# VectorE's sum of an attention output's two halves, moved ahead of the tail copy and the score passes of its step

## The chip, the cores and the metric

The kernel runs on one core of a Trainium2 chip. The metric is the device time of one execution in microseconds (us). Five engines work side by side, each through its own list of instructions in order: PE (TensorE, matmuls; its weight loads are listed as PEld), DVE (VectorE), ACT (ScalarE), POOL (GpSimd) and SP (SyncE, which issues the DMAs).

## What is computed

Attention with a learned position bias over 4 batches and 8 heads, 576 positions of 64 dimensions, then two feed-forward stages over the 2304 resulting rows of 512. Everything is float32.

```python
scores = scale * np.matmul(q, k.transpose(0, 1, 3, 2))
...
scores = scores + bias.transpose(2, 0, 1)[None, :, :, :]
scores = scores - np.max(scores, axis=-1, keepdims=True)
attn = np.exp(scores)
attn = attn / (np.sum(attn, axis=-1, keepdims=True) + 1e-09)
return np.matmul(attn, v).astype(np.float32)
...
h = np.maximum(np.maximum(x @ w1, x @ w2), x @ w3)
return (h @ w_out).astype(np.float32)
...
h = x @ w_in
g = np.where(h > 0.0, h, alpha * (np.exp(np.minimum(h, 0.0)) - 1.0))
return (g @ w_out).astype(np.float32)
```

## The kernel before

The program has four stretches: the bias table (up to about 48 us), attention (about 48 to 300 us), the first feed-forward stage (to about 620 us) and the second.

Attention goes through 16 pairs of a head pair and a batch, `n`. Each pair takes five steps `c` = 0 to 4, one for each block of query rows: four blocks of 128 rows for both heads, then a last step in which the 64 remaining rows of both heads share 128 partitions. Step number `s` is 5 `n` + `c`. Rows are called here by `c`: step c0, step c1 and so on.

In a step, PE multiplies queries and keys into two PSUM tiles `pb` (`unit_qk`, L240 and L245, one tile for each head). DVE adds the bias, takes the row minimum and writes the scores `e_t` with its minima `st_t` (`scores`, L255, one pass for each head, so two passes in steps c0 to c3 and one in c4). ACT takes the exponential in place (`expo`, L261). Two steps later PE transposes that block in 64-row pieces (`trans`, L299) into the two PSUM tiles `tq`, and ACT copies these out to SBUF (`evac`, L80); in the steps in which the block is c0 or c2, DVE copies the second of the two (L82, 128x512). The last 64 columns of a block are "tails": they are transposed into the edges of the first `pb` tile, ahead of the step's queries times keys, and DVE copies them out (`evac_tails`, L82, 128x128 or 64x128). The row sums of a half are inverted on DVE (`recip`, L276 and L277), transposed on PE, and copied out on DVE (`rows_out`, L283).

The products with the values (`pv`, L366, L370, L374) are collected in two PSUM tiles `xo`, over a half of the pair: blocks 0 and 1 (256 rows), or blocks 2, 3 and 4 (320 rows). The two `xo` tiles hold two halves of one sum. When a half is complete, ACT copies the first tile to SBUF (`x_copy`, L388, tile `xf`), DVE adds the second to it (`x_sum`, L392), and POOL multiplies by the inverted row sums (L393) and splits the result into two parts (L78, L86). PE may write the second `xo` tile for the next half only after DVE has added it. The sum of the 256-row half stands in step c2, that of the 320-row half in step c0 of the next pair.

Between these, `pump` issues pieces of the decoding of the later stages' weights, four pieces for each pair (in every step but c1): DVE operations L468, L471, L473, L475, L478 in turn, ACT operations L470 and L80 (`w_t`, `sp`), and a POOL subtraction.

The order on every engine is that in which the program issues its instructions. A list `plan` holds each call with a key, the step number plus an offset, and the calls are issued in the order of the keys (`at`, and the loop at its end). Within a step the keys that matter here are: queries times keys at .00 and .01, the tail copy at .015, the copy of the inverted sums at .016, the passes over the scores at .02 and .03, the inversion at .025, decoding at .32, and exponentials and copies of `tq` from .38 to .40. `x_sum` is at `X_AT` + 0.427 = 6.027 of the step that completed the half, so at .027 of a step.

Of the kernel before, what the change touches and what calls it, by code (L numbers as in the profile page):

```python
# [38 lines left out]
X_AT = {1: 5.6, 4: 5.6}  # L39
# [15 lines left out]
def fused_kernel(ctx, tc, tkq, vv, lt, pk, wm1, wo1, win2, wo2, out):  # L55
# [79 lines left out]
    with ExitStack() as pro:  # L135
# [57 lines left out]
        for A in range(36):  # L193
# [20 lines left out]
            c, r = divmod(A, 8)  # L214
# [381 lines left out]
    def at(key, fn, *args):  # L596
        plan.append((key, len(plan), fn, args))

    for s, (n, c) in enumerate(steps):
        o = {nm: s + off for nm, off in OFF.items()}  # L600
        at(o["qk0"], unit_qk, s, 0)
        at(o["t0"], scores, s, 0)
        at(o["ex0"], expo, s, 0)
        if c < 4:
            at(o["qk1"], unit_qk, s, 1)
            at(o["t1"], scores, s, 1)
            at(o["ex1"], expo, s, 1)
        if c in (1, 4):
            at(s + 1.025, recip, s)
            at(s + (2.205 if end else 1.995), sums, s)  # L610
            at(s + (2.312 if end else 2.016), rows_out, s)
        at(o["tr"], trans, s)
        end = s > NS - 3
        at(s + 1.98, places, s)
        at(s + (2.20 if end else 1.99), tails, s)
        at(o["ev0"], evac, s, 0)
        at(o["ev1"], evac, s, 1)
        at(s + (2.311 if end else 2.015), evac_tails, s)
        if c in (1, 4):
            for off, k in PV_AT[c]:  # L620
                at(s + off + 0.01 * k, pv, s, k)
            at(s + R_AT, load_r, s)
            at(s + X_AT[c], x_copy, s)
            at(s + X_AT[c] + 0.427, x_sum, s)
            at(s + X_AT[c] + 0.5, x_hi, s)
            at(s + X_AT[c] + 0.75, x_lo, s)
        if s > 5 and c != 1:
            at(o["pump"], pump)
        if n % 4 == 3 and n < 15:
            at(s + 0.45, load_b, n // 4 + 1, c)  # L630
# [122 lines left out]
    def small(tag, bufs):  # L753
        return mp.tile([128, NB], F32, tag=tag, name=f"{tag}_t", bufs=bufs)
# [61 lines left out]
    with tc.manual_schedule():  # L816
        for n, u in enumerate(units + [None]):
# [6 lines left out]
            if n < 2:  # L824

                for i in range(2):
                    w = take_w(("wi", u[1], 3 * i))
                    v = take_w(("w3", pre[1], i)) if pre else None
                    for q, (b, d) in enumerate(((B11, B21), (B12, B22))):
# [3 lines left out]
                        c = small("c", 4)  # L833
# [121 lines left out]
```

## Time and profile before

| | |
|---|---|
| time, median of 3 runs | 989.96 us (989.78 to 994.21) |
| the profiled execution's own time | 990.71 us |
| its span, first to last instruction | 988.9 us |
| mean granted TensorE clock | 0.998 |
| busy over the span: PE, DVE, ACT, POOL | 98%, 68%, 52%, 32% |
| busy in 142.3 to 158.0 us, one pair of attention (15.7 us): PE, DVE, ACT | 15.51, 12.56, 12.59 us |

The profile is of one execution. Its time lies 1.8 us over its span, since the span leaves out what is ahead of the first and behind the last instruction. PE's busy time counts matmuls with modelled ends, which lie over one another; a PE that is called busy may still be held up. In attention PE, DVE and ACT are all used for most of the time, and behind it PE alone sets the pace.

### The profile page before, as it was taken

To read this page: it belongs to the slowest core of one execution; us is meant where nothing else is said; L and a number is where in the kernel's file an instruction comes from. 1 tells how busy PE (TensorE), PEld (TensorE's weight loads), DVE (VectorE), ACT (ScalarE), POOL (GpSimd) and SP (SyncE) were. 2 spreads that over 40 slices of the span, in tenths; PEclk is the share of its full clock that TensorE was granted. 3 is DMA by queue.
4 is the path that set the end of the run, shared out by engine and by line. 5 is a ranking of instruction groups with operands and counts; after the bars stand their busy time and mean duration, and the time that the engine had idled before them with its cause. 6 is when DMAs were issued, how large, how long until landed. Compare 5 with 4: busy or idle time off the path is not lost.

```text
span 988.9 us, 19965 instructions
## 1 busy us (share of the span) xinstructions
PE 969.5 (98%) x7492; PEld 820.6 (83%) x7492; DVE 675.6 (68%) x1374; ACT 516.1 (52%) x1076; POOL 320.9 (32%) x307
## 2 busy tenths in 40 slices
PE   7989999999999999999999999999999999999998
PEld 4656666666658999999999999989899998989996
DVE  8968788888784899878978933745763456643342
ACT  8877778777872433334333324443454434444343
POOL 0003333334333555435534520322323233222322
PEclk9999999999999999999999999999999999999999
DMA  7965756657534468789978961465567655676563
GB/s 243 303 213 161 222 180 216 191 159 243 149 102 136 174 184 301 247 296 329 311 262 277 323 224 43 127 185 184 186 212 236 200 181 179 205 245 198 177 190 106
DMA packets 80416, 205.23 MB, mean 208 GB/s; under 512 B 13360, under 2 KB 29504, under 8 KB 80320
## 3 DMA queue, kind: packets, MB, share of 16 engines
q1 hardware_dynamic: 80320, 203.96, 63.3%
q8 instruction: 59, 0.97, 0.4%
q14 instruction: 37, 0.30, 0.1%
HBM read 155.21 MB, written 48.72 MB: 206 GB/s over the span
## 4 chain that ended last, share of the span: by engine, by line
PE 92%; DVE 3%; DMA 2%; ACT 2%; issue 0%; POOL 0%; SPq 0%; ACTq 0%
PE xo L750 18%; PE pb L794 13%; PE pb L574 12%; PE xo L366 8%; PE tq L794 7%; PE pb L240 6%; PE xo L574 5%; PE tq L574 5%; PE pb L674 4%; PE tq L299 3%; PE xo L674 2%; PE tq L674 2%; DMA scr<-o_t 2%; PE pb L299 2%; PE xo L370 2%; PE pb L204 1%
## 5 line engine op out<-in xcount | busy, mean ns | idle before, releaser
L86 POOL TENSOR_TENSOR gl<-t_t,gh 128x384 fp32r<-128x384 f32 x96 | 108.8, 1144 | 286.0 <-ACT gh L80 286.0
L261 ACT ACTIVATE e_t<-e_t,st_t 128x576 f32<-128x576 f32 x144 | 111.3, 773 | 54.3 <-DVE st_t L255 46.2
L794 PE MATMUL pb<-w_t,gh 128*128 128x512 f32 x384 | 119.3, 392 | 0.0
L574 PE MATMUL pb<-xh,w_t 128*128 128x384 f32 x448 | 116.9, 336 | 0.0
L750 PE MATMUL xo<-tt,w_t 128*128 128x384 f32 x528 | 107.4, 338 | 0.0
L255 DVE CUSTOM_DVE_ANT_0 e_t<-pb,b_t 128x576 f32<-128x576 f32 x144 | 105.0, 744 | 2.3 <-ACT o_t L213 2.1
L772 ACT ACTIVATE t_t<-c_t 128x384 f32<-128x384 f32 x96 | 50.0, 521 | 103.5 <-DVE c_t L763 95.8
L750 PEld LDWEIGHTS xo<-tt,w_t 128*128 128x128 f32 x528 | 95.0, 188 | 7.5
L366 PE MATMUL xo<-p,tv_t 64*64 64x320 f32 (+1 forms) x1024 | 96.7, 418 | 2.2 <-DVE xf L392 1.5
L393 POOL TENSOR_TENSOR xf<-xf,r_t 128x256 f32<-128x256 f32 (+1 forms) x32 | 25.7, 804 | 222.4 <-DVE xf L392 204.2
L750 PE MATMUL xo<-xh,w_t 128*128 128x384 f32 x328 | 94.6, 335 | 0.0
L574 PEld LDWEIGHTS pb<-xh,w_t 128*128 128x128 f32 x448 | 81.2, 188 | 0.5 <-issue 0.4
L240 PE MATMUL pb<-kq_t 64*128 64x288 f32 x512 | 77.5, 422 | 0.4 <-DVE st_t L255 0.4
L794 PEld LDWEIGHTS pb<-w_t,gh 128*128 128x128 f32 x384 | 70.5, 188 | 6.6
L794 PE MATMUL pb<-w_t,gl 128*128 128x512 f32 x192 | 75.5, 393 | 0.0
L574 PE MATMUL pb<-xl,w_t 128*128 128x384 f32 x224 | 75.3, 336 | 0.0
L80 ACT ACTIVATE p<-tq 128x512 f32<-128x512 f32 (+1 forms) x128 | 62.9, 529 | 8.1 <-PE xo L299 4.2
L299 PEld LDWEIGHTS tq<-ident,e_t 64*128 64x128 f32 x1152 | 48.6, 140 | 22.1 <-ACT p L80 13.2
L80 ACT ACTIVATE gh<-t_t 128x384 fp32r<-128x384 f32 x96 | 48.5, 519 | 33.4 <-DVE t_t L780 33.4
L366 PEld LDWEIGHTS xo<-p,tv_t 64*64 64x64 f32 x1024 | 38.1, 132 | 33.4 <-DVE xf L392 16.6
L750 PEld LDWEIGHTS xo<-xh,w_t 128*128 128x128 f32 x328 | 60.2, 188 | 3.0
L780 DVE SCALAR_TENSOR_TENSOR t_t<-t_t,c_t 128x384 f32<-128x384 f32 x96 | 58.5, 627 | 4.5 <-ACT t_t L773 4.1
(133 smaller groups left out, 2157.0 us busy)
## 6 DMA issues: line engine op xcount, KB each, us to landing
w_t<-scw_w SPq DMA_DIRECT2D x90, 512.0 KB
w_t<-scw_wi SPq DMA_DIRECT2D x74, 512.0 KB
kq_t<-tkq SPq DMA_DIRECT2D x16, 864.0 KB
scw_wi<-sp SPq DMA_DIRECT2D x26, 512.0 KB
scw_w<-sp SPq DMA_DIRECT2D x22, 512.0 KB
raw<-wo SPq DMA_DIRECT2D x22, 512.0 KB
scr<-o_t SPq DMA_DIRECT2D x36, 295.5 KB
raw<-wm SPq DMA_DIRECT2D x18, 512.0 KB
```

The source lines that it names most:

```text
L80: nc.scalar.activation(dst, src, AF.Copy)
L86: e.tensor_tensor(out=dst, in0=src, in1=hi.bitcast(F32), op=ALU.subtract)
L240: mm(PB[h][:, 224 + 288 * r:512 + 288 * r], t[H64[r], q0:q0 + 128], t[H64[r], 288 * h:288 * h + 288], start=True, stop=True)
L255: nc.vector.tensor_tensor_reduce(out=E[s][:, 576 * h:576 * h + 576], in0=PB[h][:, 224:800], in1=BT[n // 4, c, h], op0=ALU.add, op1=ALU.min ...
L261: nc.scalar.activation(e, e, AF.Exp, bias=st[:, h:h + 1], scale=-1.0, accum_out=SM[half(s)][:, j:j + 1])
L299: nc.tensor.transpose(dst, src[H64[g]], ident2[H64[g]])
L366: mm(XO[g][H64[h], 0:w], v[H64[g], 128 * k + 64 * h:128 * k + 64 * h + 64], ps[0][H64[g], 4 * h + k, :], start=(k == 0), stop=(k == 3 and ...
L574: mm(ps[blk][:, 0:NB], wt[:, ks], xt[:, kk, t0:t0 + NB], start=(j == 0), stop=(j == 11))
L674: mm(ps[blk][:, 0:NB], WO[0][:, kk, wt, ms], xt[:, bs], start=(j == 0), stop=(j == 3 * NM1 - 1))
L750: mm(ps, w[wt][:, ks], b[xt][:, kk], start=(start and j == 0), stop=(stop and j == 5), skip_group_check=True)
L780: pend.append([lambda: nc.vector.scalar_tensor_tensor(out=t, in0=t, scalar=-1.0, in1=c, op0=ALU.add, op1=ALU.max), last])
L794: mm(acc[t], g[:, ts], w[k], start=(f == 0 and i == 0 and j == 0), stop=(f == NU - 1 and i == 1 and j == 2))
```

## The change

One offset changes: 0.427 becomes 0.412, so that `x_sum` is issued at .012 of its step instead of .027.

```diff
             at(s + X_AT[c], x_copy, s)
-            at(s + X_AT[c] + 0.427, x_sum, s)
+            at(s + X_AT[c] + 0.412, x_sum, s)
             at(s + X_AT[c] + 0.5, x_hi, s)
```

`x_sum` also issues POOL's multiplication; POOL's list has nothing in between, and it stays the same. So do those of PE, ACT and SP. On DVE 30 of the 32 sums move.

DVE in a step c0 (the one that begins at 140 us in the trace of before). `p_2215` is the SBUF tile that takes the transposes, `p_2216` the one for the tails, `xo_901` the second of the two `xo` tiles.

```order
 L82 COPY p_2215<-tq_899 128x8x64
+L392 TENSOR_TENSOR xf<-xo_901,xf 128x320
 L82 COPY p_2216<-pb_100 128x128
 L255 ISA e_t,st_t<-pb_100,b_t 128x576
...
 L276 TENSOR_SCALAR sm_t<-sm_t 128x5
 L277 RECIPROCAL sm_t<-sm_t 128x5
-L392 TENSOR_TENSOR xf<-xo_901,xf 128x320
 L255 ISA e_t,st_t<-pb_101,b_t 128x576
 L255 ISA st_t 128x1
```

The sum moves ahead of four pieces of work: the tail copy, the first pass over the scores, and the two instructions of the inversion.

DVE in the step c2 that follows it (146.6 us in the trace of before), with the 256-row sum.

```order
 L255 ISA e_t,st_t<-pb_101,b_t 128x576
 L255 ISA st_t 128x1
+L392 TENSOR_TENSOR xf<-xo_901,xf 128x256
 L82 COPY p_2353<-pb_100 128x128
 L255 ISA e_t,st_t<-pb_100,b_t 128x576
...
 L276 TENSOR_SCALAR sm_t<-sm_t 128x4
 L277 RECIPROCAL sm_t<-sm_t 128x4
-L392 TENSOR_TENSOR xf<-xo_901,xf 128x256
 L255 ISA e_t,st_t<-pb_101,b_t 128x576
 L255 ISA st_t 128x1
```

The same move; the sum now stands directly behind the last pass over the scores of the step before.

## Rows read from the trace of the kernel before

**Rows 1.** The page: busy time, share of the span and instructions of each engine.
```profile
PE 969.5 (98%) x7492; PEld 820.6 (83%) x7492; DVE 675.6 (68%) x1374; ACT 516.1 (52%) x1076; POOL 320.9 (32%) x307
```

**Rows 2.** Line L392: who waited for it, us in total, times.
```profile
PEld xo L366: 16.6, 29
```

**Rows 3.** Timeline: start us, us, engine, line, operation [idle before it <- who ended it].
```profile
299.07 0.43 ACT L388 ACTIVATE xf<-xo 128x320 f32<-128x320 f32 x1
...
299.54 0.49 DVE L392 TENSOR_TENSOR xf<-xo,xf 128x320 f32<-128x320 f32 x1 [0.42 <-ACT xf L388]
```

**Rows 4.** Timeline of ACT in one pair of attention.
```profile
140.96 0.43 ACT L388 ACTIVATE xf<-xo 128x320 f32<-128x320 f32 x1
141.97 0.77 ACT L261 ACTIVATE e_t<-e_t,st_t 128x576 f32<-128x576 f32 x1 [0.59 <-DVE sm_t L276]
...
142.75 1.06 ACT L80 ACTIVATE p<-tq 128x512 f32<-128x512 f32 x2
...
147.81 0.38 ACT L388 ACTIVATE xf<-xo 128x256 f32<-128x256 f32 x1
...
153.25 1.06 ACT L80 ACTIVATE p<-tq 128x512 f32<-128x512 f32 x2
...
155.36 0.78 ACT L261 ACTIVATE e_t<-e_t,st_t 128x576 f32<-128x576 f32 x1 [0.29 <-DVE st_t L255]
...
156.61 0.42 ACT L388 ACTIVATE xf<-xo 128x320 f32<-128x320 f32 x1
```

**Rows 5.** Timeline of DVE in the same pair.
```profile
140.91 0.29 DVE L82 COPY p<-pb 128x128 f32<-128x128 f32 x1
...
142.10 0.45 DVE L392 TENSOR_TENSOR xf<-xo,xf 128x320 f32<-128x320 f32 x1
142.47 0.75 DVE L255 CUSTOM_DVE_ANT_0 e_t<-pb,b_t 128x576 f32<-128x576 f32 x1
...
143.14 0.91 DVE L478 TENSOR_TENSOR t_w<-t_w,x_t 128x512 int32<-128x512 int32 x1
144.51 0.28 DVE L82 COPY p<-pb 64x128 f32<-64x128 f32 x1 [0.46 <-PE pb L240]
...
147.44 0.29 DVE L82 COPY p<-pb 128x128 f32<-128x128 f32 x1 [1.11 <-PE pb L240]
...
148.62 0.39 DVE L392 TENSOR_TENSOR xf<-xo,xf 128x256 f32<-128x256 f32 x1
...
149.60 0.51 DVE L468 TENSOR_SCALAR x_t<-raw 128x512 int32<-128x512 int32 x1
150.03 0.68 DVE L82 COPY p<-tq 128x512 f32<-128x512 f32 x1
151.21 0.29 DVE L82 COPY p<-pb 128x128 f32<-128x128 f32 x1 [0.51 <-PE pb L240]
...
154.30 0.29 DVE L82 COPY p<-pb 128x128 f32<-128x128 f32 x1 [0.91 <-PE pb L245]
```

**Rows 6.** Timeline of PE's weight loads (PEld) in the same pair.
```profile
142.60 0.62 PEld L366 LDWEIGHTS xo<-p,tv_t 64*64 64x64 f32 x12 [0.64 <-DVE xf L392]
```

**Rows 7.** Timeline of PE in the same pair.
```profile
145.12 1.09 PE L366 MATMUL xo<-p,tv_t 64*64 64x256 f32 x16
...
151.49 0.66 PE L299 MATMUL tq<-ident,e_t 64*128 64x64 f32 x16
152.07 1.31 PE L366 MATMUL xo<-p,tv_t 64*64 64x320 f32 x16
```

**Rows 8.** Timeline of DVE and ACT: pieces of other pairs that differ.
```profile
94.21 0.43 ACT L388 ACTIVATE xf<-xo 128x320 f32<-128x320 f32 x1
...
102.64 0.77 DVE L475 SCALAR_TENSOR_TENSOR t_w<-raw,t_w 128x512 int32<-128x512 int32 x1
...
108.01 0.62 ACT L80 ACTIVATE w_t<-t_w 128x512 fp32r<-128x512 f32 x1
...
111.83 0.66 DVE L471 TENSOR_SCALAR t_w<-raw 128x512 int32<-128x512 int32 x1
```

## The prediction

> **What bounds the kernel now.** I read the page first: PE is busy for 98% of the span and DVE for 68% [rows 1], so whatever holds PE up is paid in full unless another engine's loop sets the pace. Then I asked who waits for the line that moves. PE's weight loads for the next half's products wait 29 times for the sum, 16.6 us in all [rows 2], some 0.57 us each. So the sum is on PE's path in nearly every half. Last I read the timelines of one pair of attention [rows 4 to 7]. It repeats every 15.65 us: the copy ahead of the 320-row sum starts at 140.96 and again at 156.61 [rows 4]. The reader is to see there that in each stretch a different engine ends the wait: in step c0 DVE's passes over the scores release ACT (0.59 us of idle time at 141.97), in c1, c2, c3 and c4 PE's queries times keys release DVE's tail copy (0.46, 1.11, 0.51 and 0.91 us of idle time) [rows 5], and in c0 and c2 the sum releases PE.
>
> **What moves, and what it runs into.** Nothing is added; the sum takes 0.45 or 0.39 us wherever it stands [rows 5]. But it needs ACT's copy of the first `xo` tile, and that copy is late: it ends at 140.96 + 0.43 = 141.39 in c0 and at 147.81 + 0.38 = 148.19 in c2 [rows 4], while DVE's tail copy starts at 140.91 and 147.44 [rows 5]. Before, tail copy and first pass filled that time, and the sum never waited. Ahead of them it must wait for ACT, and everything behind it on DVE waits too: tail copy, first pass, the two instructions of the inversion, second pass. How closely a sum follows its copy is seen where it did wait: 299.07 + 0.43 = 299.50, start at 299.54 [rows 3], so 0.04 us.
>
> **Step c0, by hand.** The sum starts at 141.39 + 0.04 = 141.43 instead of 142.10, and ends at 141.88. PE was ready for it at 142.60 - 0.64 = 141.96 [rows 6], so PE's wait is gone there: the gain of the change. The next instruction starts 0.37 us after the sum's start (142.10 to 142.47) [rows 5], so the tail copy starts at 141.80 instead of 140.91, 0.89 late. The first pass and, behind it, the exponential at 141.97 are 0.89 late too; nothing covers that, since ACT stood idle for exactly that pass. Behind the exponential in ACT's list stand the two copies of the transposes: 142.75 + 0.89 = 143.64, with an end 1.06 later, at 144.70 [rows 4]. PE's next transposes go into the tiles which these empty, so they can't be complete before about 145.07 (144.75 for the second tile and some 0.3 us of transposes), and only then come the value products that stood at 145.12 [rows 7]. So PE gets 0.05 us of the 0.64 us that it saved; the rest is a wait for ACT's copies in its place. The inversion's transposes wait for DVE meanwhile, which this longer wait hides.
>
> DVE itself: the second pass is late by 0.89 - 0.37 = 0.52 us, the decoding piece ends at 143.14 + 0.91 + 0.52 = 144.57 [rows 5], and c1's tail copy starts there instead of at 144.51. Its 0.46 us of idle time covers nearly all of the delay. About 0.05 us goes on to c1's exponentials and to the copy at 147.81.
>
> **Step c2.** The copy ends at 148.19 + 0.05 = 148.24, the sum starts at 148.28 instead of 148.62 and is followed 0.31 us later (its 0.39 less the 0.08 by which DVE's next instruction overlaps, as with 0.45 and 0.37 above), at 148.59, by the tail copy of 147.44: 1.15 late. The second pass is 0.84 late, so is the decoding piece (149.60), and so is DVE's copy of the second transposed tile: 150.87 to 151.55 instead of 150.03. PE's transposes in c3 (151.49, their second at about 151.53) [rows 7] write that tile; they go on at 151.55 + 0.05 = 151.60, 0.07 late. (The 0.05 is that between the sum's end at 142.55 and PE's load at 142.60.) Again PE has lost what it saved on the sum. With a longer decoding piece (0.77 at 102.64 against 0.51) [rows 5, 8] it is 0.26 more: 0.33 late. DVE's tail copy in c3 starts behind that copy, at 150.87 + 0.60 = 151.47, 0.26 late (0.52 with the longer piece), and ACT's copies at 153.25 with it; PE's delay from these is covered in the next c0, where it had 0.64 us to spare. In c4 the tail copy waits for PE (0.91 idle), so it is late by 0.07 (0.33), then the exponential at 155.36 and the copy for the next sum at 156.61. Where ACT has a decoding piece between (108.01) [rows 8], that copy directly follows c3's work and is late by the 0.52.
>
> So the new loop is: copy on ACT, sum, pass over scores, exponential, copies of transposes, PE, copy on ACT. **The sum.** The decoding pieces go through five patterns over five pairs. Per five pairs: 5 x 0.05 from c0; 2 x 0.02 and 1 x 0.28 added from c2 with a short and a long piece; 2 x 0.47 where ACT's own list is the limit; 0.3 for the two pairs whose copy comes later already (94.21 is 0.20 later than 140.96 less three times 15.65, another by half of that); less 2 x 0.26 where c0's piece is shorter (0.66 at 111.83 against 0.91) [rows 5, 8]. That is 1.3 us, 0.26 a pair. Some 14 pairs run between the first such copy that matters, at 78 us (140.96 less four times 15.65), and the last at 299 us [rows 3]: 3.6 us. Behind attention PE runs without gaps and gives nothing back. The profiled execution took 990.71 us, 0.75 over the median; to the median the sum is 989.96 + 3.6 = 993.6 us.
>
> The bounds: the handovers (0.04, 0.05) and the overlap of 0.08 stand about ten times in the loop, so 0.3 us a pair either way is possible, 4.2 us: 989.4 to 997.8.
>
> **One rule against this.** The Trainium skill (Perfetto Trace Analysis, section Optimization Strategy) advises to find the gaps on the engine being optimised, see what blocks it there, and make that dependency start sooner. By it the change is right. The rows agree that the gap is there 29 times; whether the time comes out, that rule does not say, and it is the first rival below.
>
> **Rivals.** *Faster.* PE gets its waits back, because the late exponentials and copies don't hold its transposes: 989.96 - 16.6 = 973.4 us [rows 2] if in both steps, 982 if in half of them. For it: PE is the busiest engine, and DVE and ACT have idle time in each pair. Against: in c0 ACT's two copies would have to be ready some 0.6 us sooner than 144.70, and the rows show no idle time ahead of them that could shrink. It decides at c1's transposes. Chance 0.12.
>
> *Nothing.* The sum no longer waits so long, because ACT comes to its copy earlier as its own list shifts; the two waits trade evenly: 990 us. Chance 0.10.
>
> *Much slower.* The delays of DVE (0.52 in c0, 0.84 in c2) are not covered by the idle time behind them, because that idle time is PE's lateness, and PE, held up in its transposes between their first and second tile, is late too. If all of it is paid: 1.36 x 14 = 19 us, 1009 us; with half, 999.5 us. It decides at c1 and c3: it needs PE to come to its queries times keys later than before in both. Chance 0.23.
>
> *My forecast*, a small loss of 0 to 8 us: 0.55.
>
> **How the numbers follow.** A measurement of this kernel tells 0.5%, 5 us, from no change. The forecast lies within it mostly (0.41 of its 0.55) and beyond it else (0.14). So faster 0.12, same 0.41 + 0.10 = 0.51, slower 0.14 + 0.23 = 0.37. The range takes all of the forecast and of nothing, the lower half of much slower, and a little of faster: 984 to 1004 us.
>
> **What would show it.** Right: all 29 PE waits for L392 small or gone; DVE idle 0.6 to 0.9 us in c0 and 1.9 us in c2 ahead of the sum, ended by ACT L388; new waits of PE's transposes for ACT's copies in c1 and DVE's copy in c3; pairs of about 15.9 us. The exponential in c0 later against the pair's start by 0.9. Wrong: pairs of 15.1 us or less with PE free of waits, or of 16.5 and more.

## The result and the profile after

The changed kernel takes 1002.08 us (median of 4 runs, 1000.05 to 1003.51), the kernel before 989.87 us (median of 4, 989.15 to 994.21). The ratio is 1.0113, 95% interval 1.0079 to 1.0147; here and below a ratio is estimated from all runs of both kernels and need not be the quotient of the two medians. The change costs 11.2 us by the ratio (0.0113 times 989.87) and 12.2 us by the medians, where 3.6 us were forecast. The profiled execution took 1001.77 us with a span of 1000.0 us.

Line L392 in the trace after: what its own engine idled for, and who waited for it (us, times; the counterpart of [rows 2]).

```profile
  ACT xf L388: 41.0, 31
...
  PEld xo L366: 3.8, 15
```

PE's wait for the sum fell from 16.6 to 3.8 us. In its place DVE now stands idle 41.0 us ahead of 31 sums, for ACT's copy. Timeline of DVE after, in the pair that answers to [rows 5]:

```profile
144.42 0.49 DVE L392 TENSOR_TENSOR xf<-xo,xf 128x320 f32<-128x320 f32 x1 [0.60 <-ACT xf L388]
144.83 0.28 DVE L82 COPY p<-pb 128x128 f32<-128x128 f32 x1
...
146.66 1.23 DVE L478 TENSOR_TENSOR t_w<-t_w,x_t 128x512 int32<-128x512 int32 x1
147.82 0.27 DVE L82 COPY p<-pb 64x128 f32<-64x128 f32 x1
...
151.52 0.43 DVE L392 TENSOR_TENSOR xf<-xo,xf 128x256 f32<-128x256 f32 x1 [1.88 <-ACT xf L388]
151.86 0.28 DVE L82 COPY p<-pb 128x128 f32<-128x128 f32 x1
...
153.68 0.66 DVE L468 TENSOR_SCALAR x_t<-raw 128x512 int32<-128x512 int32 x1
154.26 0.68 DVE L82 COPY p<-tq 128x512 f32<-128x512 f32 x1
154.86 0.27 DVE L82 COPY p<-pb 128x128 f32<-128x128 f32 x1
...
157.86 0.29 DVE L82 COPY p<-pb 128x128 f32<-128x128 f32 x1 [0.84 <-PE pb L245]
```

ACT after, in the same pair [rows 4]:

```profile
143.96 0.43 ACT L388 ACTIVATE xf<-xo 128x320 f32<-128x320 f32 x1
145.88 0.78 ACT L261 ACTIVATE e_t<-e_t,st_t 128x576 f32<-128x576 f32 x1 [1.49 <-DVE sm_t L276]
...
146.65 1.06 ACT L80 ACTIVATE p<-tq 128x512 f32<-128x512 f32 x2
...
151.11 0.38 ACT L388 ACTIVATE xf<-xo 128x256 f32<-128x256 f32 x1
...
160.17 0.42 ACT L388 ACTIVATE xf<-xo 128x320 f32<-128x320 f32 x1
```

PE's weight loads after, with the new waits ([rows 6] had the old one):

```profile
144.85 0.74 PEld L366 LDWEIGHTS xo<-p,tv_t 64*64 64x64 f32 x16
...
147.28 0.14 PEld L299 LDWEIGHTS tq<-ident,e_t 64*128 64x128 f32 x1 [0.17 <-ACT p L80]
147.76 0.32 PEld L299 LDWEIGHTS tq<-ident,e_t 64*128 64x128 f32 x7 [0.35 <-ACT p L80]
...
152.00 0.73 PEld L366 LDWEIGHTS xo<-p,tv_t 64*64 64x64 f32 x12 [0.27 <-DVE xf L392]
...
154.59 0.14 PEld L299 LDWEIGHTS tq<-ident,e_t 64*128 64x128 f32 x1 [0.46 <-ACT p L80]
154.99 0.57 PEld L299 LDWEIGHTS tq<-ident,e_t 64*128 64x128 f32 x15 [0.27 <-DVE p L82]
```

The reader is to see the predicted chain: the sum 0.03 us behind ACT's copy (143.96 + 0.43 = 144.39), the exponential of c0 behind it with 1.49 us of idle time on ACT, and PE's transposes waiting for ACT's copies in c1 and for DVE's copy in c3. In c0 PE no longer waits for the sum (144.85); in c2 0.27 us of that wait is left (152.00). One wait was not forecast: in c3 PE first stands 0.46 us for ACT's copy of the first tile (154.59), and only then 0.27 us for DVE's copy of the second. But the pair is longer than forecast: 143.96 to 160.17 is 16.21 us here. Over 13 pairs (sums of c0 from 78.08 to 293.18) it is 16.55 us on average, against 15.65 before (79.49 to 282.96): 0.89 us a pair, 11.6 us over these 13, which is the whole loss (the two spans lie 11.1 us apart). Forecast were 0.26.

The piece that had another length than forecast is the decoding piece. L478 in c0 takes 1.23 us, not the 0.91 of [rows 5]; L468 in c2 takes 0.66, not 0.51. Over the same 13 pairs the first decoding piece behind each sum went from 0.81 to 1.18 us on average in c0 and from 0.69 to 0.89 in c2. What lies beside it is POOL's work on the sum. POOL before:

```profile
142.63 0.87 POOL L393 TENSOR_TENSOR xf<-xf,r_t 128x320 f32<-128x320 f32 x1 [5.98 <-DVE xf L392]
143.59 0.78 POOL L78 TENSOR_SCALAR xh<-xf 128x320 fp32r<-128x320 f32 x1
144.45 0.87 POOL L86 TENSOR_TENSOR xl<-xf,xh 128x320 fp32r<-128x320 f32 x1
```

POOL after:

```profile
144.99 0.86 POOL L393 TENSOR_TENSOR xf<-xf,r_t 128x320 f32<-128x320 f32 x1 [6.27 <-DVE xf L392]
145.94 0.46 POOL L78 TENSOR_SCALAR xh<-xf 128x320 fp32r<-128x320 f32 x1
146.48 0.86 POOL L86 TENSOR_TENSOR xl<-xf,xh 128x320 fp32r<-128x320 f32 x1
```

After, the piece starts at 146.66, behind the start of POOL's last subtraction (146.48 to 147.34), and ends 0.55 us after that subtraction. Before, it began at 143.14 within the multiplication (to 143.50) and ended 0.55 us after that; then it was POOL's L78 that took longer, 0.78 us instead of 0.46. So in these rows the operation that starts first runs at its own length, and the other is put off. The Trainium skill (SBUF — State Buffer, section Who interferes with whom) says that a VectorE instruction with two SBUF inputs contends with a GpSimd instruction that reads SBUF, and that issue order decides who blocks. The trace agrees with both for L478, which reads two tiles in SBUF. The piece in c2, L468, reads one tile and grew too (0.51 to 0.66 us), which the first of the two does not cover.

### The profile page after: what moved, and what is told of

It is laid out like the page before. It is cut to its first block, busy times and chain, and to the rows that moved or that the text cites. A ratio compares the mean times of both kernels' runs of the same rounds, so it can differ in the third digit from the quotient of the medians.

```text
span 1000.0 us, 19980 instructions
## 1 busy us (share of the span) xinstructions
PE 972.4 (97%) x7492; PEld 823.3 (82%) x7492; DVE 679.6 (68%) x1374; ACT 516.2 (52%) x1076; POOL 315.3 (32%) x307
## 4 chain that ended last, share of the span: by engine, by line
PE 77%; DVE 11%; ACT 8%; DMA 1%; issue 1%; SPq 0%; ACTq 0%; DVEq 0%
PE xo L750 18%; PE pb L794 13%; PE pb L574 12%; PE tq L794 7%; PE xo L574 5%; PE tq L574 5%; DVE e_t L255 5%; ACT e_t L261 4%; PE pb L674 4%; PE xo L366 3%; ACT p L80 3%; DVE p L82 2%; PE pb L204 2%; PE xo L674 2%; PE tq L674 2%; PE pbb L204 2%
## 5 line engine op out<-in xcount | busy, mean ns | idle before, releaser
L366 PE MATMUL xo<-p,tv_t 64*64 64x320 f32 (+1 forms) x1024 | 85.7, 418 | 2.1 <-ACT xf L388 0.7
L299 PEld LDWEIGHTS tq<-ident,e_t 64*128 64x128 f32 x1152 | 50.9, 140 | 39.4 <-ACT p L80 21.0
L240 PE MATMUL pb<-kq_t 64*128 64x288 f32 x512 | 79.9, 427 | 0.5 <-DVE st_t L255 0.5
L299 PE MATMUL tq<-ident,e_t 64*128 64x64 f32 x1152 | 62.5, 229 | 12.1 <-DVE p L82 8.6
```

The lines of the kernel that those rows point to most:

```text
L240: mm(PB[h][:, 224 + 288 * r:512 + 288 * r], t[H64[r], q0:q0 + 128], t[H64[r], 288 * h:288 * h + 288], start=True, stop=True)
L299: nc.tensor.transpose(dst, src[H64[g]], ident2[H64[g]])
L366: mm(XO[g][H64[h], 0:w], v[H64[g], 128 * k + 64 * h:128 * k + 64 * h + 64], ps[0][H64[g], 4 * h + k, :], start=(k == 0), stop=(k == 3 and ...
```

## The experiments

Two theories stood against each other. L: a loop through the late copy on ACT, made longer by the decoding pieces that POOL's split now puts off. W: each moved sum costs DVE its wait for ACT, wherever it stands. The first edit below is shown against the kernel before, the others against the changed kernel unless said; the time beside each result is that of the kernel before, run in the same round.

**One half of the change at a time.** `only_c0`:

```diff
-            at(s + X_AT[c] + 0.427, x_sum, s)
+            at(s + X_AT[c] + (0.412 if c == 4 else 0.427), x_sum, s)
```

> Only the 320-row sum (step c0) moves; the 256-row sum (c2) keeps its old place. Theory L (a loop: late copy on ACT, sum, passes, exponentials, copies, PE, next copy; plus decoding pieces on DVE that run 0.34 us longer in c0 and 0.21 us longer in c2, since POOL's split of the result lies over them now): the loop needs both sums at the front. With the old place in c2, the sum there stands behind the first pass, about 0.4 us after its copy has ended, and takes up the delay of c0. Within 4 us of before, 986 to 994 us. Theory W (each moved sum costs DVE its wait for ACT, wherever it stands): about half of the 12 us, 994 to 998 us.

Measured: 992.05 us against 990.86, ratio 1.0015 (0.9999 to 1.0030): no change that can be told. `only_c2` has `c == 1` in that line.

> Only the 256-row sum (step c2) moves. Theory L: the delay of c2 reaches PE through DVE's longer way to the copy of the second transposed tile, and comes to c0 as a late tail copy; of about 0.6 us a pair (0.3 from the wait and 0.2 from the longer decoding piece) most stays: 994 to 999 us. Theory W: half of the 12 us as in the other half, 994 to 998 us; the two halves then add up to the whole, while L has nearly all of it here.

Measured: 998.51 us against 990.86, ratio 1.0075 (1.0057 to 1.0093). The halves are unequal, as L says and W does not. Whether they add up to the whole the times can't tell, since the intervals are as wide as the difference. By the profiles' pairs they don't: 15.76 us in only_c0 and 16.25 in only_c2 are 0.11 and 0.60 over 15.65, together 0.71 of the 0.89. In only_c0, DVE still waits for ACT 12.5 us in all ahead of its sums, and that costs nothing that can be told:

```profile
139.54 0.49 DVE L392 TENSOR_TENSOR xf<-xo,xf 128x320 f32<-128x320 f32 x1 [0.60 <-ACT xf L388]
...
141.78 1.23 DVE L478 TENSOR_TENSOR t_w<-t_w,x_t 128x512 int32<-128x512 int32 x1
...
146.78 0.39 DVE L392 TENSOR_TENSOR xf<-xo,xf 128x256 f32<-128x256 f32 x1
```

The decoding piece is put off there too (1.23 us). The sum in c2, at its old place, waits for nothing and takes up the delay.

**The late copy.** `early_after` is the changed kernel with this:

```diff
-PV_AT = {1: [(4.5, 0), (4.5, 1), (5.5, 2), (5.5, 3), (5.5, 4)],
-         4: [(3.5, 0), (3.5, 1), (4.5, 2), (4.5, 3), (5.5, 4)]}
-X_AT = {1: 5.6, 4: 5.6}
+PV_AT = {1: [(4.5, 0), (4.5, 1), (5.32, 2), (5.32, 3), (5.32, 4)],
+         4: [(3.5, 0), (3.5, 1), (4.5, 2), (4.5, 3), (5.32, 4)]}
+X_AT, C_AT = {1: 5.6, 4: 5.6}, {1: 5.39, 4: 5.386}
...
-            at(s + X_AT[c], x_copy, s)
+            at(s + C_AT[c], x_copy, s)
```

> The changed kernel, but ACT's copy for the 256-row sum is issued ahead of c1's second exponential (its products with the values are issued earlier in the program too; PE's list stays the same). The copy comes about 0.76 us sooner, the exponential behind it 0.3 us later. Theory L: DVE's wait ahead of the sum in c2 falls from 1.88 to about 1.1 us, and of the 0.76 us of the loop most comes back each pair: 990 to 996 us. A theory by which the order on DVE itself costs the time (the passes stand behind the sum) and not the late copy: 1000 to 1003 us.

Measured: 991.33 us against 990.86, ratio 1.0000 (0.9986 to 1.0014). DVE's order is that of the changed kernel, and its wait in c2 is shorter:

```profile
148.18 0.42 DVE L392 TENSOR_TENSOR xf<-xo,xf 128x256 f32<-128x256 f32 x1 [1.13 <-ACT xf L388]
```

1.88 us became 1.13, and the loss of 11 us is gone: the pairs take 15.79 us on average instead of 16.55, so that the whole 0.75 us comes back in each. So DVE's order alone does not cost the time; the copy in c2 lies on the loop. The decoding pieces are as long here as in the changed kernel (1.18 us in c0, 0.91 in c2), so this run does not say what they cost.

**POOL's split.** `small_after` (and `small_before`, with the same edit on the kernel before) does POOL's three operations on 16 columns of each result only, so most of the attention output is left out. Two added instructions of POOL fill the outputs with zeros.

```diff
+    for z in (XH, XL):
+        nc.gpsimd.memset(z.bitcast(F32), 0.0)
...
-        nc.gpsimd.tensor_tensor(out=XF[s], in0=XF[s], in1=RT.pop(s), op=ALU.mult)
+        nc.gpsimd.tensor_tensor(out=XF[s][:, 0:16], in0=XF[s][:, 0:16], in1=RT.pop(s)[:, 0:16], op=ALU.mult)
...
-        hi_of("p", x_where(s)[0], XF[s])
+        hi_of("p", x_where(s)[0][:, 0:16], XF[s][:, 0:16])
...
-        lo_of("p", xl, XF.pop(s), xh)
+        lo_of("p", xl[:, 0:16], XF.pop(s)[:, 0:16], xh[:, 0:16])
```

> The kernel before, but POOL's three operations on each result (multiplication, high part, low part) are done on 16 of its 256 or 320 columns; the rest of the attention output is left at zero, set once ahead. Theory L: DVE's decoding pieces in c0 and c2, which take 0.84 and 0.68 us here, fall to some 0.6 and 0.5 us, but they lie ahead of idle time of DVE: 986 to 992 us. A theory by which POOL's work has no bearing on DVE's pieces: they keep their length, 989 to 992 us.

> The changed kernel with the same cut of POOL's work as in small_before, so that the sum's new place is tried without POOL's split over DVE's pieces. Theory L with both costs: the pieces fall from 1.18 and 0.89 us to 0.6 and 0.5 us, and the loss against small_before is the loop's alone, 2 to 6 us, instead of 11 to 12. If the wait alone makes the loss (rival): 10 to 12 us over small_before as with all of POOL's work.

Measured: small_before 999.06 us (992.01 to 1001.48) and small_after 1004.13 us, against 991.25 (ratios 1.0069, 1.0042 to 1.0096, and 1.0134, 1.0098 to 1.0170). The level of small_before was missed: its first sum of c0 stands at 89.61 us, ten later than before's 79.49. The two fills on POOL lie ahead of it, and DVE's step of the inversion on 128x5 stood 8.36 us beside them, where it takes 0.17 in the kernel before (L276 at 141.79):

```profile
57.14 7.78 POOL L228 MEMSET xh<- 128x9216 f32 x1 [52.74 <-DMA b_t<-scr]
...
64.30 8.36 DVE L278 TENSOR_SCALAR sm_t<-sm_t 128x5 f32<-128x5 f32 x1
...
64.86 7.78 POOL L228 MEMSET xl<- 128x9216 f32 x1
```

So the two are compared with each other. The loss is 5.1 us by the medians, where the changed kernel lost 12.2, and by the spacing of the c0 sums (15.72 and 16.05 us on average over 13 pairs) 0.34 us a pair instead of 0.89. In small_after the pieces keep their own length:

```profile
151.07 0.49 DVE L394 TENSOR_TENSOR xf<-xo,xf 128x320 f32<-128x320 f32 x1 [0.60 <-ACT xf L390]
...
152.24 0.22 POOL L86 TENSOR_TENSOR xl<-xf,xh 128x16 fp32r<-128x16 f32 x1
153.30 0.69 DVE L480 TENSOR_TENSOR t_w<-t_w,x_t 128x512 int32<-128x512 int32 x1
```

The same wait of 0.60 us, the same piece (L478, here L480), 0.69 us instead of 1.23. With small_before's spread of 9 us the split between the two costs by time is good to a few us, not closer. In small_before most pieces fell to 0.69 or 0.42 us as expected, but L471 (here L473) rose to 1.53 us. The traces show why: with its split so short, POOL comes sooner to its own decoding subtraction (`w_t`, 128x512), and this starts 0.03 us ahead of that piece. In small_after the same subtraction falls on the inversion in two of every five pairs. First small_before, then small_after:

```profile
121.92 1.27 POOL L86 TENSOR_TENSOR w_t<-t_w,w_t 128x512 fp32r<-128x512 f32 x1
121.95 1.52 DVE L473 TENSOR_SCALAR t_w<-raw 128x512 int32<-128x512 int32 x1
```

```profile
119.45 1.27 POOL L86 TENSOR_TENSOR w_t<-t_w,w_t 128x512 fp32r<-128x512 f32 x1
119.68 1.07 DVE L278 TENSOR_SCALAR sm_t<-sm_t 128x5 f32<-128x5 f32 x1
```

In the other pairs of small_after, 8 of the 13, a pair takes 15.90 us on average, against 15.65 in small_before's pairs without that collision: 0.25 us. The pairs of the changed kernel with the same pieces take 16.60, 0.95 over before. So in these pairs 0.70 of the 0.95 us goes with POOL's split, and 0.25 stays with the loop. That is more than the pieces had grown against the kernel before, since in both small kernels they are shorter than they were there (0.69 us against 0.77 to 0.91). Shorter pieces alone gain nothing: those pairs of small_before take the 15.65 us of before.

**Other places for the sum.** `behind_pass` has `0.422` where the kernel before has 0.427: behind the first pass, ahead of the inversion.

> Both sums stand behind the first pass over the scores, ahead of the inversion (offset 0.422). Theory L: at 141.79 in c0 and 148.31 in c2 of the trace of before the copy on ACT has already ended (141.39 and 148.19), so the sum waits for nothing, the passes keep their times, the second pass too, and PE's wait for the sum falls from 0.64 and 0.57 us by about 0.3 each: 14 pairs times 0.2 to 0.6 us, 981 to 987 us. Theory W: also no wait and so no loss, but no statement on a gain; 985 to 991 us. A theory by which PE's wait for the sum costs nothing: 989 to 991 us.

Measured: 983.45 us against 990.86, ratio 0.9926 (0.9904 to 0.9948): faster than both kernels. DVE, PE's loads and POOL there, in c0:

```profile
139.71 0.48 DVE L392 TENSOR_TENSOR xf<-xo,xf 128x320 f32<-128x320 f32 x1
...
140.25 0.62 PEld L366 LDWEIGHTS xo<-p,tv_t 64*64 64x64 f32 x12 [0.37 <-DVE xf L392]
...
141.05 0.69 DVE L478 TENSOR_TENSOR t_w<-t_w,x_t 128x512 int32<-128x512 int32 x1
...
141.23 0.82 POOL L78 TENSOR_SCALAR xh<-xf 128x320 fp32r<-128x320 f32 x1
```

The sum waits for nothing, PE waits 0.37 instead of 0.64 us, and the decoding piece starts ahead of POOL's next operation, so that it keeps its 0.69 us, and it is POOL's L78 that takes longer (0.82 us). In all PE's loads wait 8.8 us for the sum instead of 16.6, and those 7.8 us are about the 7.4 that the kernel gains; the shorter pieces gained nothing in small_before.

**The idle time filled.** `gap_after` is the changed kernel with the decoding pieces of c0 and c2 ahead of the sum:

```diff
-            at(o["pump"], pump)
+            at(s + (0.011 if c in (0, 2) else 0.32), pump)
```

> The changed kernel, with the decoding pieces of c0 and c2 issued ahead of the sum instead of behind the second pass: they fill the time in which DVE waits for ACT's copy, and POOL's split no longer lies over them. Theory L: DVE's idle time ahead of the sum falls by a piece's length, the copy of the second transposed tile in c2 comes 0.6 to 0.9 us sooner, and c1's tail copy 1.2 us: 984 to 992 us. Theory W (the wait for ACT costs, whatever stands in it): 998 us and more.

Measured: 980.26 us against 991.25, ratio 0.9905 (0.9872 to 0.9939). W is refuted once more: DVE still waits 25.0 us for ACT ahead of 22 sums, and the kernel is faster than before. How much of this comes from the filled idle time and how much from pieces out of the way of POOL's split, this run does not separate. In the rows a piece takes up c0's wait, and c2's is left:

```profile
136.25 0.68 DVE L478 TENSOR_TENSOR t_w<-t_w,x_t 128x512 int32<-128x512 int32 x1
136.93 0.49 DVE L392 TENSOR_TENSOR xf<-xo,xf 128x320 f32<-128x320 f32 x1
...
143.34 0.42 DVE L392 TENSOR_TENSOR xf<-xo,xf 128x256 f32<-128x256 f32 x1 [1.69 <-ACT xf L388]
```

`gap_early` adds early_after's edit.

> Both cures together: the decoding pieces of c0 and c2 ahead of the sum (as in gap_after), and ACT's copy for the 256-row sum ahead of c1's second exponential (as in early_after). Theory L: in c2 DVE idles 1.7 us for the copy in gap_after; a copy 0.76 us sooner gives back 0.3 to 0.7 us a pair as far as c2 lies on the loop: 971 to 977 us. If c0's loop alone (copy, sum, first pass, exponential, copies of transposes) sets the pace by then: 979 to 981 us.

Measured: 978.87 us against 989.48, ratio 0.9895 (0.9879 to 0.9912): hardly more, near the second case of its expectation, in which c0's loop sets the pace. `mix_early` differs from it in c0 alone, where the sum stands behind the first pass and the decoding piece at its old place (new lines only):

```diff
+            at(s + C_AT[c], x_copy, s)
+            at(s + X_AT[c] + (0.412 if c == 1 else 0.422), x_sum, s)
...
+            at(s + (0.011 if c == 2 else 0.32), pump)
```

with early_after's tables.

> In c0 the sum behind the first pass (as in behind_pass); in c2 the sum first, the decoding piece ahead of it, and ACT's copy sooner. Theory L: c0 keeps its exponential's time and c2's sum waits only shortly, so both losses are gone and PE's wait is 0.3 us in c0 and near 0 in c2: 970 to 977 us. If c2's passes, about 0.4 us later for the sum that stands ahead of them, set the pace: 980 to 985 us.

Measured: 973.14 us against 989.48, ratio 0.9839 (0.9822 to 0.9855), the fastest of all. That 5.7 us come from c0 alone bears out that c0's loop held gap_early. In c2 the sum still stands ahead of its copy here, and DVE waits 0.53 to 0.80 us for it in nearly every pair.

## Why the prediction was right, and where it was off

*The direction and the loop were right.* Each step shows in the rows after: the tail copy 0.41 us behind the sum's start (forecast 0.37), the decoding piece 2.24 us behind it in c0 and 2.16 in c2 (143.66 - 141.43 = 2.23 and 150.44 - 148.28 = 2.16 by the prediction's numbers), PE's wait for the sum gone in c0 and replaced there by ACT's copies, in c3 by DVE's copy of the second tile. The exponential of c0 is 0.90 us late (forecast 0.9), DVE waits 1.88 us in c2 (1.9) and in c0 0.60 us in three of five pairs, 1.06 and 1.16 in the others (0.6 to 0.9), and of PE's 29 waits for the sum 15 are left, at 0.25 us each.

*The term that was mis-sized* is the decoding piece in "Step c0, by hand" and "Step c2": 143.14 + 0.91 + 0.52 in c0, and in c2 the copy behind the piece at 150.87 (0.26 later with a longer piece), took the piece at its old length. It runs 0.37 us longer in c0 and 0.20 us longer in c2, on average. With the forecast's 0.26 from the loop that makes 0.83 of the 0.89 us a pair. The 0.26 itself is near the 0.25 that small_after kept in its pairs without the collision. In the pair shown, c1's tail copy comes 3.40 us behind the sum (147.82 - 144.42) instead of 144.57 - 141.43 = 3.14, and copy to copy it is 7.15 + 9.06 us, against 6.90 + 8.82 forecast. The remaining 0.06 us a pair is about what the sums take more: 0.49 and 0.43 us, where the prediction had 0.45 and 0.39 "wherever it stands". The one row of a sum that waited ([rows 3]) had shown the 0.49. This adding up is an argument from lengths; no run changes the pieces' length alone. (In the prediction's sum 0.91 - 0.66 is 0.25, not 0.26, which changes nothing.)

*The bounds* were drawn from handovers alone and ended at 997.8 us; a length that depends on what another engine does beside it was not among them. By the prediction's own sign of being wrong, pairs of 16.5 us and more, its own forecast did not hold: they take 16.55, and the loss lies beyond its 0 to 8 us. The range held, by luck in part, because of the rival "much slower", but that rival gave another mechanism (PE late at its queries times keys in both c1 and c3), which is not what happened: c1's tail copy at 147.82 followed DVE's own piece, c3's at 154.86 DVE's own copy, both with no idle time for PE.

*The first rival*, PE's waits given back, fell for the changed kernel, by the reason given: nothing ahead of ACT's copies in c0 could shrink. But making PE's dependency start sooner did pay once the sum in c0 moved only as far as its own input allowed: behind_pass gives 7 us, mix_early 16.

## What to carry to other kernels

When a step moves ahead in an engine's list, look first at its latest input: beyond that point the engine stands still, and every instruction behind it is late by the difference. The end of the input's producer against the start of the row it is moved past tells that before anything is built. Such a wait costs time only where what stands behind it is on the loop: in mix_early c2's sum still waits, and that kernel is the fastest. And an idle time that takes up the delay of one move need not take up that of two: one half of this change cost nothing that can be told, the other 7.4 us, both 11. And when an instruction of VectorE shifts against GpSimd's work on the same result, its length in the old trace is no longer its length.

## What was not expected of the hardware

The same integer operation of 128x512 on DVE (L478) took 0.69 us alone (small_after), 0.91 beside a multiplication on POOL that had begun before it, and 1.23 beside a subtraction that had begun 0.18 us before it; where it began first (behind_pass), it took 0.69 and POOL's 0.46 us operation took 0.82. So the two engines delayed each other by up to 0.5 us an instruction on tiles that they do not share. It can be far more: in small_before a DVE instruction on five columns stood through the end of one fill on POOL and the whole of the next, 8.36 us, though its start (64.30) lies ahead of the second fill's (64.86).
